# Two layers of windowed attention and a squared-ReLU MLP: products of scores and of maxima no longer ordered behind readers of other banks of their tile

## The chip, the core and the metric

The kernel runs on one core of a Trainium2 chip. The metric is the device time of one execution in microseconds (us), lower is better; three executions are shown for the kernel before, and profiled executions of its program give the views that are read here. Five engines work side by side, each through its own instructions in order: TensorE (PE, its weight loads shown apart as PEld), VectorE (DVE), ScalarE (ACT), GpSimd (POOL) and SyncE (SP), which here issues nearly all transfers. They wait for each other at semaphores.

## The reference

Input x has 2048 rows of 640. Four blocks follow each other: A, B, A, B, each added to x.

```
A: y = layernorm(x); q, k, v = split(y @ wqkv), 32 heads of 20
   s = (q @ k^T) * 20 ** -0.5, kept where 0 <= row - column < 256, else -1e9
   x = x + (softmax(s) @ v) @ wo
B: y = layernorm(x); h = relu(y @ w1 + b1); x = x + (h * h) @ w2 + b2     (w1: 640 x 1536)
```

Block A and block B of one pass are a layer of the kernel.

## The kernel before, in words

The 2048 rows are cut into 8 groups of 256 and there are two layers, so there are 16 units, numbered u in order; unit 8 is the first group of the second layer. The keys and values that a unit's rows may see are its own and those of the group before it. Units 0 and 8 have no group before them, and so have less attention work.

Products with weights (called dense here, all through `mm3`, L149) take each operand as a high and a low float16 part, and three products for each chunk of 128. They fill accumulators of one bank in the partial-sum memory (two buffers, tag `mm`), which ACT and DVE empty.

Attention goes by quads of four heads, eight quads a unit. Two kinds of turns use the other six banks, as two tiles of three banks (`banks`, tag `bb`, one for each half e of the partitions):

- A turn of maxima (`max_quad`, L282) forms the scores of a quad, 18 products (L308), and DVE adds the mask and takes row maxima in eight instructions (L321, a reduction and the read of its accumulator each). Banks 0, 1 and 2 hold w = 0, 1, 2; the products of w = 3 lie in the last 128 columns of all three banks, and are read last.
- A turn of scores (`exp_quad`, L345) forms the transposed scores less their maxima, 16 products (L359) in three steps, one bank of each tile for a step; ACT takes the exponential of each bank (L366, six a turn, into `pt`). GpSimd then clears what the window excludes (L376, L380). Units 0 and 8 have two steps and eight products.

Products of exponentials and values (`pv_quad`, L393, products L405) follow, in an `mm` buffer. ACT copies the result (L416), DVE and POOL divide by the sum, ACT and DVE split it in two parts `ot` (L426, L427), and SP writes these to memory (L431).

`together` (L547) writes out the order of TensorE by hand: for each quad a turn of scores, a share of dense products (0.55 of what belongs to the quad), a turn of maxima for a quad five further on, the products with the values, and the rest of the dense products. The dense products of an inner unit u are, in this order: q and k of unit u+1 (`stage_qk`), the output projection of unit u-1 (`stage_o`), v of unit u+1, and the MLP of unit u-1 (`stage_f`). TensorE keeps the order in which the program is written (L587). The order on the other engines is found by a scheduler that simulates the program, with some work preferred (`first`, L87).

Row maxima become rows of `qt` by way of a transpose on TensorE (L329), two DVE instructions and eight small transfers (L340). The normalised rows of `stage_o` become the left operand `y2` of the MLP by a cast on ACT (L214, `yl`), a subtraction on DVE (L215) and four transposing transfers (L217).

Dependencies between instructions are derived from the tiles that they touch. All products of a turn go into the same two tiles that ACT or DVE reads meanwhile.

## Time and profile before

| | us |
|---|---|
| median of three runs | 2677.45 |
| lowest, highest | 2673.51, 2682.87 |
| the profiled execution | 2666.85 |
| its span, first to last instruction | 2665.0 |
| TensorE busy in it | 2097.6 |
| VectorE, ScalarE, GpSimd busy | 1124.1, 810.4, 728.6 |

A busy time is the time in which at least one instruction of the engine runs. [...] Idle time of an engine is put down to whatever ended it. The first turn of scores of unit 0 starts at 119.2 us, and units 6, 8 and the last turn of scores are at 1026.1, 1348.6 and 2580.9 us.

### The profile page before, as it was taken

What the parts mean: (1) busy time and instruction counts of PE and PEld (TensorE: products, weight loads), DVE (VectorE), ACT (ScalarE), POOL (GpSimd) and SP (SyncE); (2) the same over time, 40 slices, a digit from 0 to 9 for tenths busy, and PEclk for the clock granted to TensorE, in tenths of its full rate; (3) what the DMA queues carried; (4) which work ended last, traced back from release to release, by engine and by line L of the source; (5) the groups of instructions that cost most, each with busy time, mean ns of one, the idle gap of its engine ahead of it and who ended that gap; (6) DMA issues with size and microseconds to landing.
All of it is one profiled execution on the core that took longest, in us unless ns stands there. A gap on an engine that the chain in (4) does not pass through costs nothing.

```text
span 2665.0 us, 45823 instructions
## 1 busy us (share of the span) xinstructions
PE 2097.6 (79%) x17542; PEld 1343.8 (50%) x17542; DVE 1124.1 (42%) x3473; ACT 810.4 (30%) x1716; POOL 728.6 (27%) x1434
## 2 busy tenths in 40 slices
PE   5777777877878788778888778787787877878688
PEld 4444445545554455445555555455544554545356
DVE  5554444343343443434445443434434334343422
ACT  5443223223232232332323232232322323223241
POOL 4333223223131231322322132231312223222241
PEclk9888888888888888888998888888888888888789
DMA  7540031130311302213141311403113022130100
GB/s 204 142 108 22 16 85 28 47 88 23 80 33 46 88 16 63 60 36 87 31 105 33 87 29 45 90 23 85 28 46 87 16 79 44 46 78 11 41 24 26
DMA packets 239069, 154.91 MB, mean 58 GB/s; under 512 B 80640, under 2 KB 219776, under 8 KB 238848
## 3 DMA queue, kind: packets, MB, share of 16 engines
q1 hardware_dynamic: 230432, 142.46, 21.8%
q10 hardware_dynamic: 8416, 9.51, 1.3%
q8 instruction: 138, 2.26, 0.4%
q14 instruction: 83, 0.68, 0.1%
HBM read 82.58 MB, written 52.43 MB: 51 GB/s over the span
## 4 chain that ended last, share of the span: by engine, by line
PE 61%; ACT 11%; DVE 10%; issue 9%; DMA 5%; SPq 3%; POOL 2%; ACTq 0%; DVEq 0%; POOLq 0%
PE acc L149 41%; PE pv L405 10%; ACT pt L366 7%; PE bb L359 5%; PE bb L308 4%; DVE bb L321 3%; SPq L340 2%; DVE mx L321 2%; DMA xt<-xs 1%; DMA stg<-in_B_w_dram 1%; ACT hh L497 1%; ACT r L493 1%; DVE bst L161 1%; ACT yl L214 1%; DMA stg<-in_A_wo_dram 1%
## 5 line engine op out<-in xcount | busy, mean ns | idle before, releaser
L321 DVE CUSTOM_DVE_ANT_0 bb<-bb,maskb 128x384 f32<-128x384 f32 (+2 forms) x1024 | 523.0, 559 | 301.4 <-PE bb L308 298.3
L366 ACT ACTIVATE pt<-bb 128x512 f32<-128x512 f32 x736 | 392.9, 586 | 206.5 <-PE bb L359 204.2
L308 PE MATMUL bb<-kt,qt 60*128 60x128 f16 (+1 forms) x2176 | 216.1, 245 | 272.9 <-DVE mx L321 270.0
L359 PE MATMUL bb<-qt,kt 62*128 62x128 f16 (+1 forms) x1920 | 212.8, 258 | 245.3 <-ACT pt L366 241.4
L423 POOL TENSOR_TENSOR po<-po,rb 128x256 f32<-128x256 f32 x128 | 93.2, 728 | 1117.9 <-DVE rb L422 1081.3
L149 PE MATMUL acc<-y,w_s 128*128 128x256 f16 x2880 | 388.2, 302 | 1.5 <-DVE y L176 1.5
L149 PE MATMUL acc<-w_s,hh 128*128 128x320 f16 x2304 | 372.4, 326 | 0.0
L149 PEld LDWEIGHTS <-w_s 128*128 128x128 f16 x2880 | 307.0, 109 | 98.0 <-issue 35.7
L416 ACT COPY po<-pv 128x256 f32<-128x256 f32 x128 | 47.6, 372 | 1010.6 <-PE pv L405 1010.6
L149 PE MATMUL acc<-yT,wq_s 128*128 128x256 f16 x2400 | 322.0, 301 | 5.4 <-DVE yT L176 3.0
L149 PEld LDWEIGHTS <-hh 128*128 128x128 f16 x2304 | 241.0, 106 | 136.3 <-issue 25.5
L149 PEld LDWEIGHTS <-wq_s 128*128 128x128 f16 x2400 | 252.8, 108 | 87.5 <-issue 38.5
L405 PE MATMUL pv<-pt,vt 128*32 128x128 f32 (+1 forms) x3840 | 293.9, 473 | 1.7 <-DVE qd L244 1.0
L308 PEld LDWEIGHTS <-qt 60*128 60x128 f16 x2176 | 95.3, 95 | 381.1 <-issue 378.8
L359 PEld LDWEIGHTS <-kt 62*128 62x128 f16 x1920 | 87.0, 94 | 357.5 <-issue 351.5
L376 POOL TENSOR_SCALAR_AFFINE_SELECT pt<-pt 128x256 f32<-128x256 f32 x448 | 187.9, 421 | 281.3 <-ACT pt L366 274.6
L380 POOL TENSOR_SCALAR_AFFINE_SELECT pt<-pt 128x256 f32<-128x256 f32 x512 | 207.8, 411 | 40.4 <-ACT pt L366 23.8
L498 DVE TENSOR_TENSOR hh<-r,hh 128x256 f16<-128x256 f32 x192 | 84.7, 458 | 259.9 <-ACT hh L497 253.1
L405 PEld LDWEIGHTS pv<-pt,vt 128*32 128x32 f32 x3840 | 149.1, 150 | 82.8 <-issue 67.2
L149 PE MATMUL acc<-wo_s,od 128*128 128x320 f16 x960 | 162.6, 332 | 5.6 <-DMA od<-o 3.9
L149 PE MATMUL acc<-wq_s,yT 128*128 128x320 f16 x960 | 160.8, 329 | 1.1 <-ACT vt L271 0.8
L496 POOL TENSOR_TENSOR r<-r 128x256 f32<-128x256 f32 x192 | 117.8, 634 | 156.2 <-ACT r L493 155.9
(62 smaller groups left out, 1449.6 us busy)
## 6 DMA issues: line engine op xcount, KB each, us to landing
qk<-qd SPq DMA_DIRECT2D x32, 640.0 KB
qt<-qk SPq DMA_DIRECT2D x32, 480.0 KB
kt<-qk SPq DMA_DIRECT2D x32, 480.0 KB
qk<-qd SPq DMA_DIRECT2D x32, 320.0 KB
o<-ot SPq DMA_DIRECT2D x256, 40.0 KB
od<-o SPq DMA_DIRECT2D x32, 320.0 KB
stg<-in_B_w_dram ACTq DMA_DIRECT2D x30, 256.0 KB
xt<-in_A_x_dram SPq DMA_DIRECT2D x16, 320.0 KB
```

The costliest lines, as they stand in the source:

```text
L149: nc.tensor.matmul(acc, lhs(a, c), rhs(b, c), start=(k == 0), stop=(k == 3 * nk - 1))
L308: nc.tensor.matmul(to, qt[r, p, i * P:(i + 1) * P], kt[r, p, a:b], start=True, stop=True)
L321: nc.vector.tensor_tensor_reduce(out=v, in0=v, in1=mask, scale=1.0, scalar=-3.0e38, op0=ALU.add, op1=ALU.max, accum_out=accum)
L340: nc.sync.dma_start(qt[r:r + 1, 2 * GQ * G:2 * GQ * (G + 1), i * P:(i + 1) * P], mT[s0:s0 + 2 * GQ, a, :])
L359: nc.tensor.matmul(bb[e][:, k, o:o + w], kt[r, 2 * qd + j, ko:ko + P], qt[r, 2 * qd + j, q0 * P:q0 * P + w], start=True, stop=True)
L366: at[0] = nc.scalar.activation(pt[:, :o], bb[e][:, k, :o], AF.Exp, scale=SCALE / (QS * QS))
L376: nc.gpsimd.affine_select(out=m, in_=m, pattern=[[0, 2], [-1, P]], compare_op=ALU.is_gt, fill=0.0, base=0, channel_multiplier=1)
L380: nc.gpsimd.affine_select(out=m, in_=m, pattern=[[0, 2], [1, P]], compare_op=ALU.is_ge, fill=0.0, base=0, channel_multiplier=-1)
L405: nc.tensor.matmul(pv[32 * jj:32 * (jj + 1), q0 * P:(q0 + qn) * P], vf[:, c:c + 32], pj[:, j, :], start=(k == 0), stop=(k == len(steps) - ...
L423: nc.gpsimd.tensor_tensor(po, po, rb.rearrange("p a b -> p (a b)"), op=ALU.mult)
L496: nc.gpsimd.tensor_tensor(r, r, r, op=ALU.mult)
L498: nc.vector.tensor_sub(hh[:, 1, f0 + f, :], r, hh[:, 0, f0 + f, :])
```

## The change

A helper `apart` tells the framework that a given product does not depend on a list of instructions. In both kinds of turns the kernel keeps a list `read` of the readers issued so far in this turn, and calls `apart` for each product that follows. The readers in the list work in other banks of the tile than the product; the readers of the product's own bank come after it in the program. Dependencies on the tile's previous user stay. No instruction is added or removed.

```
+    def apart(ins, others):
+        for it in others:
+            tc.declare_no_dep(ins.ins, it.ins, reason="other banks")
...
-        found = []
+        found, read = [], []
...
-                    nc.tensor.matmul(to, qt[r, p, i * P:(i + 1) * P], kt[r, p, a:b], start=True, stop=True)
+                    apart(nc.tensor.matmul(to, qt[r, p, i * P:(i + 1) * P], kt[r, p, a:b], start=True, stop=True),
+                          read)
...
-                nc.vector.tensor_tensor_reduce(out=v, in0=v, in1=mask, scale=1.0, scalar=-3.0e38,
-                                               op0=ALU.add, op1=ALU.max, accum_out=accum)
+                read.append(nc.vector.tensor_tensor_reduce(out=v, in0=v, in1=mask, scale=1.0, scalar=-3.0e38,
+                                                           op0=ALU.add, op1=ALU.max, accum_out=accum))
...
-        out = []
+        out, read = [], []
...
-                        nc.tensor.matmul(bb[e][:, k, o:o + w], kt[r, 2 * qd + j, ko:ko + P],
-                                         qt[r, 2 * qd + j, q0 * P:q0 * P + w], start=True, stop=True)
+                        apart(nc.tensor.matmul(bb[e][:, k, o:o + w], kt[r, 2 * qd + j, ko:ko + P],
+                                               qt[r, 2 * qd + j, q0 * P:q0 * P + w], start=True, stop=True), read)
...
+                read.append(at[0])
```

TensorE's instructions stand in the same order before and now; only what they wait for differs. This is a turn of scores of a unit with three steps, from the last product of the first step to the first of the third; `Activation_49` is the semaphore of ACT. Before:

```order
L359 MATMUL bb<-qt,kt_79 128x256
L359 LDWEIGHTS kt_79
L359 MATMUL bb<-qt,kt_79 128x128 [waits Activation_49]
L359 LDWEIGHTS kt_79
L359 MATMUL bb<-qt,kt_79 128x128 [waits Activation_49]
...
L359 MATMUL bb<-qt,kt_77 128x128
L359 LDWEIGHTS kt_77
L359 MATMUL bb<-qt,kt_77 128x256 [waits Activation_49]
L359 LDWEIGHTS kt_77
L359 MATMUL bb<-qt,kt_77 128x256 [waits Activation_49]
```

The same products now:

```order
L365 MATMUL bb<-qt,kt_79 128x256
L365 LDWEIGHTS kt_79
L365 MATMUL bb<-qt,kt_79 128x128
L365 LDWEIGHTS kt_79
L365 MATMUL bb<-qt,kt_79 128x128
...
L365 MATMUL bb<-qt,kt_77 128x128
L365 LDWEIGHTS kt_77
L365 MATMUL bb<-qt,kt_77 128x256
L365 LDWEIGHTS kt_77
L365 MATMUL bb<-qt,kt_77 128x256
```

The four waits for ACT inside the turn are gone; the waits of the first products of the turn, for the readers of the tiles' last user, stand as they did. In a turn of maxima four waits for DVE go in the same way.

The other engines' instructions are the same in number, and stand in part in another order. On ACT, in the fourth turn of scores of unit 7 (its exponentials are `pt_11788` to `pt_11817`), before:

```order
L416 COPY po_11719<-pv_11701 128x256
L426 CAST ot_11718<-po_11719 128x2x128
L214 CAST yl_11751<-xt_11642 128x640
L271 ACTIVATE vt4_92<-acc_11760 128x16x20
L366 ACTIVATE pt_11788<-bb_11782 128x512
L366 ACTIVATE pt_11791<-bb_11783 128x512
L214 CAST yl_11751<-xt_11741 128x640
L366 ACTIVATE pt_11802<-bb_11782 128x512
L366 ACTIVATE pt_11806<-bb_11783 128x512
L366 ACTIVATE pt_11814<-bb_11782 128x512
L366 ACTIVATE pt_11817<-bb_11783 128x512
```

And now:

```order
L423 COPY po_11719<-pv_11701 128x256
L214 CAST yl_11751<-xt_11642 128x640
L271 ACTIVATE vt4_92<-acc_11760 128x16x20
L372 ACTIVATE pt_11788<-bb_11782 128x512
L372 ACTIVATE pt_11791<-bb_11783 128x512
L433 CAST ot_11718<-po_11719 128x2x128
L372 ACTIVATE pt_11802<-bb_11782 128x512
L372 ACTIVATE pt_11806<-bb_11783 128x512
L372 ACTIVATE pt_11814<-bb_11782 128x512
L372 ACTIVATE pt_11817<-bb_11783 128x512
L214 CAST yl_11751<-xt_11741 128x640
```

The second cast of `yl` moved from behind two of the six exponentials to behind all six, and the cast of `ot` from ahead of them to behind the first two. On SP, the queue of transfers of one unit, before:

```order
L217 DMA_TRANSPOSE y2_8590<-yl_8591 128x5x128 x2
L466 DMA xt_8779<-in_B_b2_dram 128x640
L217 DMA_TRANSPOSE y2_8590<-yl_8591 128x5x128 x2
L340 DMA qt_6495<-mT_8662 1x8x128 x8
...
L431 DMA o5_8176<-ot_8558 20x2x512 x4
L217 DMA_TRANSPOSE yT_9241<-yl_9242 128x5x128 x2
L431 DMA o5_8176<-ot_8970 20x2x512 x4
L217 DMA_TRANSPOSE yT_9241<-yl_9242 128x5x128 x2
```

And now:

```order
L217 DMA_TRANSPOSE y2_8590<-yl_8591 128x5x128 x2
L473 DMA xt_8779<-in_B_b2_dram 128x640
L346 DMA qt_6495<-mT_8662 1x8x128 x4
L217 DMA_TRANSPOSE y2_8590<-yl_8591 128x5x128 x2
L346 DMA qt_6495<-mT_8662 1x8x128 x4
...
L438 DMA o5_8176<-ot_8558 20x2x512 x4
L217 DMA_TRANSPOSE yT_9241<-yl_9242 128x5x128 x3
L438 DMA o5_8176<-ot_8970 20x2x512 x4
L217 DMA_TRANSPOSE yT_9241<-yl_9242 128x5x128
```

Four of the eight transfers of maxima now stand ahead of the second pair of transposes and four behind it, and one more transpose stands ahead of the second write of `ot`.

## Rows read from the trace of the kernel before

**Rows 1.** The page: busy time, share of the span and instructions of each engine.
```profile
PE 2097.6 (79%) x17542; PEld 1343.8 (50%) x17542; DVE 1124.1 (42%) x3473; ACT 810.4 (30%) x1716; POOL 728.6 (27%) x1434
```
**Rows 2.** Span and mean granted TensorE clock of the core.
```profile
core 0: 2665.0 us, clock 0.851
```
**Rows 3.** Waits: who waited for whom, us in total, times, longest.
```profile
PE bb L308 <- DVE mx L321: 270.0, 486, 4.3
...
PE bb L359 <- ACT pt L366: 241.4, 455, 3.3
```
**Rows 4.** Timeline, a turn of scores: start, us, engine, line, xcount, idle before.
```profile
1213.84 0.39 PE L359 MATMUL bb<-qt,kt 62*128 62x256 f16 x4
...
1214.32 1.08 ACT L366 ACTIVATE pt<-bb 128x512 f32<-128x512 f32 x2 [1.01 <-PE bb L359]
1214.97 0.21 PE L359 MATMUL bb<-qt,kt 62*128 62x128 f16 x1 [0.74 <-ACT pt L366]
...
1215.46 0.38 PE L359 MATMUL bb<-qt,kt 62*128 62x128 f16 x7 [0.28 <-ACT pt L366]
...
1216.55 0.27 PE L359 MATMUL bb<-qt,kt 62*128 62x256 f16 x1 [0.71 <-ACT pt L366]
...
1217.03 0.38 PE L359 MATMUL bb<-qt,kt 62*128 62x256 f16 x3 [0.22 <-ACT pt L366]
```
**Rows 5.** Timeline, a turn of maxima on TensorE and VectorE, first and last rows.
```profile
1224.03 0.51 PE L308 MATMUL bb<-kt,qt 60*128 60x128 f16 x10
1224.57 0.57 DVE L321 CUSTOM_DVE_ANT_0 bb<-bb,maskb 128x384 f32<-128x384 f32 x1 [1.84 <-PE bb L308]
...
1228.59 0.60 DVE L321 CUSTOM_DVE_ANT_0 bb<-bb,maskb 128x384 f32<-128x384 f32 x1
...
1229.10 0.60 DVE L321 CUSTOM_DVE_ANT_0 bb<-bb,maskb 128x384 f32<-128x384 f32 x1
```
**Rows 6.** Windows: busy us (x) of PE, PEld, DVE, ACT, POOL; clock, DMA share, GB/s.
```profile
1213.84:1217.34 3.50, 1.55 (x17) 0.71 (x17) 0.00 (x0) 2.17 (x4) 1.53 (x4) 1.00 0.86 280
1217.34:1221.10 3.76, 3.76 (x21) 2.74 (x21) 0.00 (x0) 1.08 (x2) 1.59 (x5) 0.55 0.54 127
1221.10:1224.02 2.92, 2.92 (x27) 2.44 (x25) 0.69 (x1) 0.60 (x1) 0.00 (x0) 1.00 1.06 169
0.00:119.20 119.20, 76.64 (x532) 52.88 (x532) 61.86 (x219) 54.53 (x106) 44.50 (x50) 0.91 0.65 177
1026.10:1194.30 168.20, 134.56 (x1127) 85.60 (x1126) 70.67 (x214) 48.58 (x102) 43.62 (x90) 0.84 0.23 54
1348.60:1391.10 42.50, 36.23 (x334) 25.89 (x335) 22.67 (x81) 11.81 (x26) 7.53 (x17) 1.00 0.54 135
1348.60:1479.00 130.40, 107.91 (x909) 73.40 (x908) 65.64 (x214) 36.56 (x86) 31.70 (x58) 0.92 0.31 70
2580.90:2665.00 84.10, 76.99 (x601) 57.45 (x600) 19.30 (x44) 14.97 (x36) 14.58 (x23) 0.97 0.11 34
```
**Rows 7.** The same view of line L308 alone: busy us of PE, PEld; clock.
```profile
1224.02:1227.53 3.51, 1.56 (x18) 0.76 (x18) 1.00 0.03 4
```
**Rows 8.** Timeline of TensorE about the start of unit 8.
```profile
1343.28 1.51 PE L405 MATMUL pv<-pt,vt 128*32 128x256 f32 x32
1344.72 3.98 PE L149 MATMUL acc<-w_s,hh 128*128 128x320 f16 x28
...
1364.66 5.09 PE L149 MATMUL acc<-yT,wq_s 128*128 128x256 f16 x45
```
**Rows 9.** Timeline of ACT ahead of a turn of scores that starts at 1314.62 us.
```profile
1312.55 0.84 ACT L493 ACTIVATE r<-acc,b1s 128x256 f32<-128x256 f32 x2 [1.89 <-PE acc L149]
...
1315.44 1.09 ACT L366 ACTIVATE pt<-bb 128x512 f32<-128x512 f32 x2
```
**Rows 10.** Waits of SP's queue: us in total, times, longest.
```profile
SPq L217 <- ACT hh L497: 373.2, 9, 43.4
```

## The prediction

> **What bounds the kernel now.** I read the shares of busy time first: TensorE is busy for 2097.6 of 2665.0 us, VectorE for 42%, ScalarE for 30% [rows 1]. So TensorE sets the time, and two things can be had from it: the 567.4 us in which it stands idle, and the clock at which it works, which is 0.851 in the mean [rows 2].

> The list of waits says where the idle time lies: 270.0 us in products of maxima that wait for VectorE, in 486 waits, and 241.4 us in products of scores that wait for ScalarE, in 455 [rows 3]. Together that is 511.4 us; 56.0 us are left for everything else. A turn of scores in the timeline shows what these waits are [rows 4]. Four products run, then the next waits 0.74 us for the first exponential and the one behind it 0.28 us for the second; then the third step waits 0.71 and 0.22 us in the same way. That is 1.95 us of idle time in a turn of 3.5 us. A unit of three steps has eight such turns with four waits each, and the number of waits fits these inner ones alone. In front of the turns there is nothing: from 1221.10 to 1224.02 TensorE is busy throughout [rows 6], and the turn of maxima starts at 1224.03 [rows 5].

> The windows show the second cost [rows 6]. In the turn of scores the clock is granted in full, 1.00, and TensorE is busy for 1.55 of 3.50 us. [...] Unit 8 is the counter-example that the kernel brings along: its turns of scores have two steps, its first turns of maxima are shorter too, TensorE is busy for 36.23 of the first 42.50 us, and the clock is 1.00 throughout. So I read the fall of the clock as a consequence of the idle time in the turns.

> **The change part by part.** The order of TensorE is the same, and the rows of the order show the four inner waits of a turn gone. Inside a turn a product then has nothing to wait for, and the 511.4 us go as far as nothing else is late in their place.

> For the clock I rebuild a unit of three steps from rows at clock 1.00. Dense products by the code: 10 groups of 15 for q and k and 12 of 15 for the first half of the MLP make 330 of 256 columns; 8 groups of 15 for v and the output projection and 4 of 36 for the second half make 264 of 320 columns. A product of 256 columns takes 5.09 / 45 = 0.113 us and one of 320 columns 3.98 / 28 = 0.142 us [rows 8], so 37.3 + 37.5 = 74.8 us. Eight turns of scores at 1.55 us [rows 6], eight of maxima at 1.56 us [rows 7] and eight products with the values at 1.51 us [rows 8] add 37.0 us. That makes 111.8 us, where unit 6 has 134.56 us of busy TensorE at a clock of 0.84, in 168.20 us [rows 6]. The ratio is 0.831.

> Over the kernel: 76.64 us of busy time belong to the start, 107.91 to unit 8 and 76.99 to the end, whose clocks of 0.91, 0.92 and 0.97 leave less to win [rows 6]. At clock 0.84 a fall of 0.16 is worth 16.9% of the busy time; in proportion 0.09 is worth 9.5%, 0.08 8.4% and 0.03 3.2%, so these become 69.4, 98.8 and 74.5 us. The other 1836.1 us times 0.831 make 1525.8. TensorE's work at the upper level is thus about 1768.5 us. With the 56.0 us of other idle time the span would be 1824.5 us if nothing else came late.

> What comes late next is the tail of the readers, which now runs into the dense work behind the turn. ScalarE: its first exponential starts 0.48 us after the turn, and six at 0.54 us [rows 4] end 3.7 us after it. The next turn of maxima needs their banks after 1.55 us of products and 0.55 of 74.8 / 8, that is 5.1 us of dense work: at 6.7 us. VectorE: its first reduction starts 0.54 us after the turn's first product and they follow each other every 0.51 us [rows 5], so eight end after about 4.7 us; the next turn of scores comes after 1.56 + 1.51 + 4.2 = 7.3 us. These 3.0 and 2.6 us of dense work are the cover. What can use it up is other work in the same queues. In unit 6 VectorE is busy for 70.67 us, of which 64 reductions take 33; ScalarE for 48.58, of which 48 exponentials take 26 [rows 6]. That leaves 4.7 and 2.8 us of other work for each quad. If all of it fell into the tails, VectorE would be 4.7 + 4.7 - 7.3 = 2.1 us late and ScalarE not at all: 16.8 us a unit. The lower bound is 0.

> The moved casts on ScalarE I cost at nothing: the dense work between turns hides them. Of the cast of `yl` that now stands behind four more exponentials, the cover is v of the next unit; if that is too short, the transposes behind it, `y2`, and the four transfers of maxima queued behind these on SP are late by up to 4 x 0.54 = 2.2 us each, once a unit: 4.4 us more. So a unit loses between 0 and 21 us to new waits. I take 5, nearer to the lower end, because the rows show no wait ahead of a turn today and the cover of 2.6 us is above half of the other work of VectorE. Over 16 units that is 80 us.

> The sum: 1824.5 + 80 = 1904.5 us of span. The profiled execution is 1.85 us above its span, and the median of the runs is 0.47% above this span; I scale by that to 1913, and forecast 1915 us. With 0 and 21 us a unit it is 1833 and 2171 us.

> [...]

> **The rivals.** First: only the waits go, and the clock stays as it is. For it: the mean clock also contains falls behind turns of maxima and products with the values, and those I have not taken apart. Against it: unit 8. Its time: 2097.6 + 56.0 + 80 = 2234 us of span, 2244 us.

> Second: the waits come back at the first product of a turn. One mechanism: ScalarE and VectorE work in order, and other work stands ahead of the readers. For it: at 1312.55 ScalarE begins with the MLP and reaches the exponentials of a turn at 1315.44, 2.9 us later and 0.8 us after the turn's start [rows 9]. Against it: the cover of 2.6 to 3.0 us. At the upper bound the time is 2171 us; with some falls of the clock kept as well, about 2200.

> Third, slower than before: SP's queue. One more transpose now stands ahead of a write of `ot`; `ot` has a single buffer, so a late write holds ScalarE's next cast, and the exponentials behind it. SP waits for such transposes by as much as 43.4 us, nine times 373.2 us in total [rows 10]. Were TensorE to pay 43.4 us in each of 12 units, 521 us would more than cancel the waits, and idle TensorE would lose the clock too: about 2690 us. It decides once SP is held for longer than the quad, some 14 us, between a write of `ot` and the next. Against it: transposes stood ahead of these writes before, and TensorE has next to no wait that leads back to them.

> That the change does nothing is excluded by the rows of the order.

> **How the numbers follow.** The forecast, waits gone and the clock up, with 0 to 14 us of new waits a unit (1833 to 2060 us), has 0.76. The second rival has 0.12, about half of it below 2170; the first 0.09; the third 0.03. The range of 1835 to 2170 us leaves out some 0.18. A measurement of this kernel tells 0.3% from no change. All but the third rival are faster, so 0.97 for faster; of its 0.03 I give 0.01 to no change and 0.02 to slower.

> **What would show it.** Right: the two waits fall from 511.4 us to under 100, what is left stands at the first products of turns, a turn of scores takes about 1.6 us, the mean clock is above 0.95, and an inner unit takes about 117 us. Only the clock wrong: turns of 1.6 us, but windows at 0.5 remain. The tails wrong: a list of waits in which the same two pairs keep hundreds of us. The third: TensorE waiting for `po`, `pt` or `kt` by tens of us at a time. A time above 2244 us would refute the whole argument.

## The result, and the profile after

The changed kernel takes 1794.42 us (median of four runs), the kernel before 2675.48 us (median of four): a ratio of 0.6705, with a 95% interval of 0.6687 to 0.6723. That is a third less time, in the direction that was forecast, and below the range that was given (1835 to 2170 us). The profiled execution has a span of 1792.0 us. One later execution of the changed kernel (2688.47 us, its clock held at 0.558) and one of the kernel before (6120.37 us) are left out of the medians and ratios below.

The page of the changed kernel, its row of engines:

```profile
PE 1616.1 (90%) x17542; PEld 1177.0 (66%) x17542; DVE 1068.6 (60%) x3473; ACT 781.2 (44%) x1716; POOL 742.0 (41%) x1434
```

Its clock, in the view that answers to [rows 2]:

```profile
core 0: 1792.0 us, clock 0.979
```

The list of waits of TensorE (us in total, times, longest us):

```profile
PE acc L149 <- DVE qd L244: 23.9, 29, 1.6
PE bb L365 <- DVE mx L327: 20.2, 23, 2.5
PE acc L149 <- DMA od<-o: 17.0, 3, 9.3
...
PE pv L412 <- ACT r L500: 10.5, 14, 1.5
...
PE bb L365 <- DVE rc L428: 7.7, 16, 1.9
...
PE bb L313 <- ACT pt L372: 4.0, 5, 1.8
```

The two pairs that held 511.4 us [rows 3] are gone: no product of scores waits for an exponential of its own turn, and no product of maxima for a reduction of its own turn. What is left stands at first products (20.2 + 7.7 us for VectorE's tail, 4.0 us for ScalarE's, and 0.9 us between turns of maxima at the start), in front of the products with the values and in the dense work. TensorE's idle time is 1792.0 - 1616.1 = 175.9 us, where it was 567.4.

The timeline of TensorE and of ScalarE through one quad of an inner unit; these rows answer to [rows 4], [rows 5] and [rows 8]:

```profile
519.04 0.83 PE L365 MATMUL bb<-qt,kt 62*128 62x256 f16 x16
519.81 4.79 PE L149 MATMUL acc<-wo_s,od 128*128 128x320 f16 x34
524.53 0.84 PE L313 MATMUL bb<-kt,qt 60*128 60x128 f16 x18
525.30 1.51 PE L412 MATMUL pv<-pt,vt 128*32 128x256 f32 x32
526.74 1.67 PE L149 MATMUL acc<-wo_s,od 128*128 128x320 f16 x11
```

```profile
519.53 3.04 ACT L372 ACTIVATE pt<-bb 128x512 f32<-128x512 f32 x6 [0.77 <-PE bb L365]
```

There is no bracket of idle time on TensorE's rows: the pieces join. The 16 products of scores take 0.83 us and the 18 of maxima 0.84 us. ScalarE's six exponentials end at 522.57, 3.53 us after the turn's start and 1.96 us ahead of the next turn: the tail lies under dense work, as the sum had it (3.7 us).

Windows of the changed kernel, columns as in [rows 6]; they are the start, units 0, 1 and 2, then unit 6, unit 8, the turns of unit 15, and the end:

```profile
0.00:110.30 110.30, 68.81 (x532) 49.90 (x532) 59.55 (x222) 53.73 (x106) 43.31 (x50) 0.90 0.71 194
110.30:176.90 66.60, 51.41 (x504) 33.02 (x504) 40.27 (x132) 38.88 (x89) 35.18 (x56) 0.90 0.43 121
176.90:279.00 102.10, 82.48 (x926) 57.39 (x925) 57.53 (x195) 40.78 (x93) 41.43 (x87) 0.90 0.13 33
279.00:387.10 108.10, 101.46 (x1124) 74.08 (x1124) 68.10 (x218) 46.89 (x102) 45.27 (x91) 0.98 0.34 83
...
702.70:808.80 106.10, 99.26 (x1125) 73.06 (x1125) 67.17 (x214) 46.89 (x102) 45.04 (x91) 1.00 0.37 85
...
911.20:1004.80 93.60, 89.89 (x909) 66.92 (x908) 61.47 (x214) 34.95 (x85) 32.58 (x57) 1.00 0.41 96
...
1635.00:1709.20 74.20, 55.15 (x629) 36.13 (x629) 34.17 (x105) 34.19 (x79) 36.13 (x77) 0.89 0.12 33
1709.20:1792.00 82.80, 75.51 (x600) 56.24 (x599) 20.87 (x47) 17.83 (x44) 17.57 (x29) 1.00 0.11 35
```

Unit 6 took 168.20 us at a clock of 0.84 [rows 6] and takes 106.10 us at 1.00, with TensorE busy for 99.26 us of it. The start, units 0 to 2 and unit 15 still lose clock (0.90, 0.90, 0.90, 0.98 and 0.89); the other units have 1.00.

Where the 873 us of span went is read from TensorE's groups (line, count, busy us, mean ns, idle before). After:

```profile
L149 PE MATMUL acc<-y,w_s 128*128 128x256 f16 x2880 | 337.4, 275 | 13.5 <-ACT r L500 8.5 <-DMA y<-yl 2.8 <-DVE y L176 1.5
L149 PE MATMUL acc<-w_s,hh 128*128 128x320 f16 x2304 | 325.7, 299 | 0.0
L149 PE MATMUL acc<-yT,wq_s 128*128 128x256 f16 x2400 | 286.5, 278 | 14.8 <-DVE qd L244 9.8 <-DVE yT L176 3.7 <-ACT po L423 1.3
L412 PE MATMUL pv<-pt,vt 128*32 128x128 f32 (+1 forms) x3840 | 194.2, 332 | 20.1 <-ACT r L500 10.5 <-POOL pt L387 7.4 <-DVE qd L244 1.7
L149 PE MATMUL acc<-wo_s,od 128*128 128x320 f16 x960 | 143.2, 305 | 32.4 <-DMA od<-o 17.0 <-DVE qd L244 13.7 <-DVE x L465 1.7
L149 PE MATMUL acc<-wq_s,yT 128*128 128x320 f16 x960 | 142.9, 300 | 16.3 <-DVE mT L339 14.7 <-ACT vt L271 1.1 <-DVE qd L244 0.3
L365 PE MATMUL bb<-qt,kt 62*128 62x128 f16 (+1 forms) x1920 | 108.3, 246 | 27.9 <-DVE mx L327 20.2 <-DVE rc L428 7.7
L313 PE MATMUL bb<-kt,qt 60*128 60x128 f16 (+1 forms) x2176 | 105.2, 237 | 5.6 <-ACT pt L372 4.0 <-DVE mx L327 0.9 <-DMA kt<-qk 0.6
```

The same groups of the kernel before:

```profile
L149 PE MATMUL acc<-y,w_s 128*128 128x256 f16 x2880 | 388.2, 302 | 1.5 <-DVE y L176 1.5
L149 PE MATMUL acc<-w_s,hh 128*128 128x320 f16 x2304 | 372.4, 326 | 0.0
L149 PE MATMUL acc<-yT,wq_s 128*128 128x256 f16 x2400 | 322.0, 301 | 5.4 <-DVE yT L176 3.0 <-DVE qd L244 2.4
L405 PE MATMUL pv<-pt,vt 128*32 128x128 f32 (+1 forms) x3840 | 293.9, 473 | 1.7 <-DVE qd L244 1.0 <-ACT r L493 0.7
L308 PE MATMUL bb<-kt,qt 60*128 60x128 f16 (+1 forms) x2176 | 216.1, 245 | 272.9 <-DVE mx L321 270.0 <-DVE bmv L163 1.1 <-DMA kt<-qk 0.4
L359 PE MATMUL bb<-qt,kt 62*128 62x128 f16 (+1 forms) x1920 | 212.8, 258 | 245.3 <-ACT pt L366 241.4 <-DMA qt<-mT 0.5 <-issue 0.2
L149 PE MATMUL acc<-wo_s,od 128*128 128x320 f16 x960 | 162.6, 332 | 5.6 <-DMA od<-o 3.9 <-DVE x L458 1.7
L149 PE MATMUL acc<-wq_s,yT 128*128 128x320 f16 x960 | 160.8, 329 | 1.1 <-ACT vt L271 0.8 <-DVE qd L244 0.3
```

| TensorE, us | before | after | less |
|---|---|---|---|
| idle | 567.4 | 175.9 | 391.5 |
| products of scores and maxima (two rows) | 428.9 | 213.5 | 215.4 |
| products with the values | 293.9 | 194.2 | 99.7 |
| dense (five rows) | 1406.0 | 1235.7 | 170.3 |

The rows add to 876.9; they overlap a little where groups join. The third and fourth rows, 270.0 us, I put down to the clock: in unit 6 the dense products and those with the values were busy for 86.98 and 21.74 us at a mean clock of 0.84, and are for 75.83 and 12.15 us at 1.00. The second row is not idle time, and only a part of it is the clock (the eight interrupted turns of scores of unit 6 took 14.33 us at its clock of 0.84, about 1.8 us each; the pieces of the turn in [rows 4], which ran at 1.00, add to 1.63 us). It is the one that the prediction had wrong.

### The profile page after: what moved, and what is told of

Read it like the earlier page. It is cut to its first block, busy times and chain, and to the rows that moved or that the text cites. A ratio compares the mean times of both kernels' runs of the same rounds, so it can differ in the third digit from the quotient of the medians.

```text
span 1792.0 us, 45770 instructions
## 1 busy us (share of the span) xinstructions
PE 1616.1 (90%) x17542; PEld 1177.0 (66%) x17542; DVE 1068.6 (60%) x3473; ACT 781.2 (44%) x1716; POOL 742.0 (41%) x1434
## 4 chain that ended last, share of the span: by engine, by line
PE 53%; DVE 19%; issue 8%; POOL 8%; ACT 6%; DMA 5%; SPq 1%; ACTq 0%; DVEq 0%; POOLq 0%
PE acc L149 41%; DVE bb L327 8%; PE pv L412 4%; ACT pt L372 4%; PE bb L365 3%; DVE mx L327 3%; PE bb L313 3%; POOL pt L387 2%; POOL pt L383 2%; DVE hh L505 2%; POOL r L503 2%; DMA qk<-qd 1%; DVE rb L426 1%; POOL po L430 1%; DVE qd L244 1%
## 5 line engine op out<-in xcount | busy, mean ns | idle before, releaser
L327 DVE CUSTOM_DVE_ANT_0 bb<-bb,maskb 128x384 f32<-128x384 f32 (+2 forms) x1024 | 512.6, 558 | 126.4 <-PE bb L313 125.3
L149 PE MATMUL acc<-y,w_s 128*128 128x256 f16 x2880 | 337.4, 275 | 13.5 <-ACT r L500 8.5
L149 PEld LDWEIGHTS <-w_s 128*128 128x128 f16 x2880 | 278.1, 98 | 75.0 <-issue 38.6
L149 PE MATMUL acc<-w_s,hh 128*128 128x320 f16 x2304 | 325.7, 299 | 0.0
L149 PE MATMUL acc<-yT,wq_s 128*128 128x256 f16 x2400 | 286.5, 278 | 14.8 <-DVE qd L244 9.8
L412 PE MATMUL pv<-pt,vt 128*32 128x128 f32 (+1 forms) x3840 | 194.2, 332 | 20.1 <-ACT r L500 10.5
L412 PEld LDWEIGHTS pv<-pt,vt 128*32 128x32 f32 x3840 | 107.9, 110 | 70.9 <-issue 28.2
L433 ACT CAST ot<-po 128x256 f16<-128x256 f32 x128 | 52.3, 408 | 228.9 <-POOL po L430 228.9
L149 PEld LDWEIGHTS <-od 128*128 128x128 f16 x960 | 92.5, 99 | 81.2 <-issue 28.0
L327 DVE DVE_READ_ACCUMULATOR2_ANT mx<- 128x1 f32 x1024 | 143.6, 140 | 0.0
L365 PE MATMUL bb<-qt,kt 62*128 62x128 f16 (+1 forms) x1920 | 108.3, 246 | 27.9 <-DVE mx L327 20.2
```

The costliest lines, as they stand in the source:

```text
L149: nc.tensor.matmul(acc, lhs(a, c), rhs(b, c), start=(k == 0), stop=(k == 3 * nk - 1))
L327: read.append(nc.vector.tensor_tensor_reduce(out=v, in0=v, in1=mask, scale=1.0, scalar=-3.0e38, op0=ALU.add, op1=ALU.max, accum_out=accum))
L365: apart(nc.tensor.matmul(bb[e][:, k, o:o + w], kt[r, 2 * qd + j, ko:ko + P], qt[r, 2 * qd + j, q0 * P:q0 * P + w], start=True, stop=True), ...
L412: nc.tensor.matmul(pv[32 * jj:32 * (jj + 1), q0 * P:(q0 + qn) * P], vf[:, c:c + 32], pj[:, j, :], start=(k == 0), stop=(k == len(steps) - ...
L433: nc.scalar.copy(oh, pf)
```

## The experiments

**One kind of turn alone.** The theory was that each interrupted turn costs its own waits and its own fall of the clock; the rival, that one interrupted turn a quad holds the clock down as much as two. The first run leaves `apart` away in the turns of maxima:

```
-                    apart(nc.tensor.matmul(to, ...), read)
+                    nc.tensor.matmul(to, ...)
```

> Only the turns of scores lose their inner waits; the turns of maxima wait as before. Theory (idle time in the turns, its pipeline tails, and a clock that falls behind each interrupted turn): the 241 us of waits for ScalarE go, the busy time of these products falls from 213 to about 108 us, and half of the 270 us that dense products and products with the values lost to the clock comes back: 2675 - 241 - 105 - 135, plus some 60 us of new waits, about 2255 us, mean clock about 0.92. Rival (one interrupted turn a quad holds the clock down as much as two): the clock stays near 0.85 and the time near 2390 us.

Measured: 2189.76 us, clock 0.908. The second leaves it away in the turns of scores:

```
-                        apart(nc.tensor.matmul(bb[e][:, k, o:o + w], ...), read)
+                        nc.tensor.matmul(bb[e][:, k, o:o + w], ...)
```

> Only the turns of maxima lose their inner waits. Theory: 270 us of waits for VectorE and about 111 us of busy time of these products go, and half of the clock's 270 us: 2675 - 270 - 111 - 135 + 60, about 2220 us, mean clock about 0.92. Rival (one interrupted turn a quad is enough for the clock): about 2355 us at a clock near 0.85. If the two halves of the change were independent, the savings of this run and of the one with scores alone would add to 881 us.

Measured: 2237.77 us, clock 0.900. Both are within 3% of the theory and 5 to 9% from the rival, and both clocks are nearer to the theory's 0.92 than to 0.85. Against 2669.82 us for the kernel before beside them they save 480 and 432 us, 912 together, where the whole change saves 881: nearly independent. TensorE's groups show which turn takes the clock from which work. With the turns of scores freed:

```profile
L411 PE MATMUL pv<-pt,vt 128*32 128x128 f32 (+1 forms) x3840 | 275.5, 444 | 6.5 <-POOL pt L386 5.0 <-DVE qd L244 1.0 <-POOL pt L382 0.3
L313 PE MATMUL bb<-kt,qt 60*128 60x128 f16 (+1 forms) x2176 | 214.2, 242 | 280.8 <-DVE mx L326 273.8 <-ACT pt L371 3.8
...
L364 PE MATMUL bb<-qt,kt 62*128 62x128 f16 (+1 forms) x1920 | 102.7, 245 | 0.5 <-issue 0.3
```

With the turns of maxima freed:

```profile
L365 PE MATMUL bb<-qt,kt 62*128 62x128 f16 (+1 forms) x1920 | 219.2, 260 | 297.9 <-ACT pt L372 274.0 <-DVE rc L428 9.7 <-DVE mx L327 6.5
L412 PE MATMUL pv<-pt,vt 128*32 128x128 f32 (+1 forms) x3840 | 184.7, 331 | 1.8 <-DVE qd L244 0.7 <-POOL pt L387 0.6 <-ACT r L500 0.5
...
L313 PE MATMUL bb<-kt,qt 60*128 60x128 f16 (+1 forms) x2176 | 106.3, 240 | 2.2 <-DVE mx L327 1.2 <-DMA kt<-qk 0.8
```

The products with the values stand right behind the turn of maxima: they stay at 275.5 us while that turn is interrupted and fall to 184.7 when it is not. The five dense groups, which stand behind both, add to 1279.6 us in the first run and 1370.3 in the second, between 1406.0 and 1235.7. So I read from these busy times that the clock falls behind the turn that idles, and comes back with it (0.908 and 0.900 in the mean, where it is 0.851 with both turns interrupted and 0.979 with none). The busy time of a turn's own products halves in the run that frees it, and only there (scores 102.7 and 219.2 us, maxima 214.2 and 106.3).

**Idle time without waits.** If idle time is what costs, it can be filled in place of being removed. This kernel has all the dependencies of the kernel before, and puts dense products between the steps of a turn:

```
+            if w < 2:
+                between(1.5e3)
...
+            if k + 1 < len(steps):
+                between(1.5e3)
...
+            fill[0] = None if after and k == 0 else more
```

Here `between` draws 1.5 us from the same generator of dense products that fills the time behind the turns. The first turn of scores of each unit, and the turns of maxima at the start, are left whole.

> The kernel before with all its dependencies, but 1.5 us of dense products are put between the steps of a turn (not in the first turn of scores of a unit), and taken from the dense work behind the turns. Theory (it is TensorE's idle time in the turns that costs, by itself and by the clock, not the dependencies as such): the readers work under the dense products, the inner waits nearly go, the clock is above 0.95 and the time is near that of the changed kernel: 1830 us (1780 to 1900). Rival (the waits cost by being there, as semaphores or through the order of the other engines): it stays above 2400 us.

Measured: 1956.67 us, clock 0.963. The rival is out, but the time is 57 us above the end of the theory's range. Its groups of turns:

```profile
L367 PE MATMUL bb<-qt,kt 62*128 62x128 f16 (+1 forms) x1920 | 180.0, 252 | 82.3 <-DVE mx L327 40.1 <-ACT pt L374 32.5 <-DMA qt<-mT 3.9
L314 PE MATMUL bb<-kt,qt 60*128 60x128 f16 (+1 forms) x2176 | 158.8, 240 | 30.9 <-DVE mx L327 17.2 <-ACT pt L374 11.7 <-DMA kt<-qk 0.8
```

The 32.5 us for ScalarE lie mostly in the first turns of scores of the units, which have no dense products in them. TensorE is idle for 195.7 us in this run (1956.0 - 1760.3), hardly more than in the changed kernel, but the products of the turns are busy for 338.8 us instead of 213.5. One of its turns of maxima, at a clock of 1.00 and with no wait in it:

```profile
704.18 0.51 PE L314 MATMUL bb<-kt,qt 60*128 60x128 f16 x10
...
706.84 0.34 PE L314 MATMUL bb<-kt,qt 60*128 60x128 f16 x4
...
708.86 0.34 PE L314 MATMUL bb<-kt,qt 60*128 60x256 f16 x4
```

The three pieces add to 1.19 us, where the whole turn takes 0.84: 0.18 us a break. In [rows 4] the five pieces add to 1.63 us, against 0.83 for the whole turn: 0.20 us a break. Over the kernel I counted pieces in the traces, a piece ending where other products follow or where TensorE stands idle: the turns are in 1202 pieces before, 280 after and 851 here. So a further piece costs 215.4 / 922 = 0.23 us before, with part of the lower clock in it, and 125.3 / 571 = 0.22 us here. My reading is that each piece has a start and an end that the next one does not share, and that breaking the turn pays them again. These are busy times of the turns' own products; where a piece joins dense work the two overlap (by 0.06 us at 519.81 us of the changed kernel: 519.04 + 0.83 - 519.81), so TensorE's own row grows by 144.2 us (1760.3 against 1616.1), the lower clock (0.963 against 0.979) included. How much of that is breaks and how much clock is not shown.

**Halves.** At the rate of the dense products, 0.113 us for 256 columns [rows 8], the 3072 columns of a turn would take 1.36 us one behind the other, by this estimate; the turn takes 0.83, and the next work starts 0.77 us after the turn's start (519.81 - 519.04). The two halves e use different partitions, so I took it that they run side by side because they alternate; in the records of this turn the 16 products start in eight pairs, the two of a pair 3 to 5 ns apart. On this theory the forecast for halves that do not alternate was about 1920 us (1880 to 1950); by the estimate above, 1.36 - 0.83 = 0.53 us more in some 240 turns make 127 us, and with the 1794 us of the changed kernel 1921 us. The first run puts e outside within each step:

```
-                for j in range(2):
-                    for e in range(2):
...
+            for e in range(2):
+                o = 0
...
+                    for j in range(2):
```

> As the changed kernel, but in a turn all products of the half e = 0 come before those of e = 1, instead of alternating. Same products, same columns. [...] Rival (the turn is short only because no product waits any more and the modelled ends are counted once): no change, 1794 us within 10.

Measured: 1798.17 us: the rival's number. But it does not show the rival's reason (the profile models the ends of TensorE's products). The turn in its timeline:

```profile
568.15 0.84 PE L313 MATMUL bb<-kt,qt 60*128 60x128 f16 x18
```

It is as short as before, and still shorter than the 1.36 us of its columns in a row. In the records of this turn the first products of the two halves start 10 ns apart, although two or three of one half stand in the program ahead of the other's each time. Over the kernel the turns are busy for 111.2 and 106.3 us, against 108.3 and 105.2. To tell the two apart the halves had to be further from each other. The next two runs write all products of a turn ahead of all its readers, with no dependency declared away; the second sorts them by half:

```
+        items = [(w, part, e) for w in (3, 0, 1, 2) for part in parts_of(w)[3] for e in range(2)]
+        items.sort(key=lambda it: it[2])        # second run alone
+        for w, (kt, a, b, c), e in items:
...
+            nc.tensor.matmul(to, qt[r, p, i * P:(i + 1) * P], kt[r, p, a:b], start=True, stop=True)
+        for w in (3, 0, 1, 2):                  # then the readers, as before
```

> The kernel before, without any call that takes a dependency away, but written so that all products of a turn come first and all its readers after them. The products stand on TensorE in the order of the changed kernel. Theory (the inner waits came only from readers that stand in the program ahead of later products of the same tile): no reader stands ahead of a product, the waits are gone, and the time is that of the changed kernel, 1794 us, plus up to 30 us if the first reader now waits for the last product (0.35 to 0.4 us later in each turn, mostly under dense work). Rival (the waits would come back another way, at the readers): above 2000 us.

For the second there were two forecasts, both against the first. Theory (with eight or nine products of one half ahead of the other's, the halves no longer run side by side): turns near the 1.36 us, and 60 to 150 us more. Rival (they run side by side over a whole turn): turns of 0.85 us, and the same time within 10 us.

> As the run with all products of a turn first, but all products of the half e = 0 of the turn stand ahead of those of e = 1. To be read against that run. In the run with the halves apart within a step alone, the trace showed the first products of both halves starting 10 ns apart, so the two halves ran side by side all the same. [...]

Measured: 1811.83 us and 1837.66 us. The first says that the order in which the program is written was the cause of the waits: written products first, the kernel before is 17 us from the changed one, with no dependency taken away. The second, timeline of a turn of maxima with one half behind the other:

```profile
572.19 1.18 PE L311 MATMUL bb<-kt,qt 60*128 60x128 f16 x18
```

1.18 us, 0.34 more than with the halves alternating, and less than the 1.36 of the columns in a row: by that estimate the halves overlap in part even there. The time grows by 26 us, which is neither the theory's 60 to 150 nor the rival's 10: part of the longer turns falls into time in which TensorE would have waited (idle 141.3 us against 181.2).

**The cover of the tails.** The share of dense work behind the turn of scores, 0.55, sets how much of it covers ScalarE's tail and how much VectorE's.

```
-    SHARE = 0.55
+    SHARE = 0.75        # other runs: 0.30, 0.45
```

> The changed kernel with 0.75 instead of 0.55 of a quad's dense work behind the turn of scores, so only 0.25 behind the turn of maxima. Theory (dense work is the cover of the readers' tails): behind a turn of maxima there are 0.84 + 1.51 + 0.25 x 9.4 = 4.7 us of TensorE, and VectorE's reductions alone end after about 4.7; with its other work it is 1 to 2 us late in some 112 turns, so the time is 1900 to 2020 us, and the waits of scores for maxima (20 us) grow to over 100. Rival (the tails are far from deciding): within 15 us of 1794.

> The changed kernel with 0.30 of a quad's dense work behind the turn of scores. Theory (cover): ScalarE's exponentials end about 3.7 us after the turn's start and TensorE comes to the turn of maxima after 0.84 + 0.30 x 9.4 = 3.7 us; with ScalarE's other work it is up to 1.5 us late, and the products with the values, which need GpSimd's part too, wait as well: 1850 to 1980 us. Rival (not deciding): within 15 us of 1794.

Measured: 1899.48 us at 0.75, and 1800.19 us at 0.30. TensorE's waits at 0.75:

```profile
PE bb L365 <- DVE mx L327: 83.5, 107, 3.0
PE bb L365 <- DVE rc L428: 52.0, 60, 3.4
```

And at 0.30:

```profile
PE pv L412 <- POOL pt L387: 35.6, 18, 2.8
PE pv L412 <- DVE qd L244: 18.7, 14, 2.6
PE bb L313 <- ACT pt L372: 16.7, 40, 1.5
```

VectorE's cover decides, as the theory had it, with a time at the lower end of its range (1900 to 2020 us): with less cover, turns of scores wait 135.5 us. For ScalarE the rival was right (within 15 us of 1794), and the theory wrong by 50 us and more: at 0.30 the turns of maxima wait 16.7 us in all, so ScalarE's other work seldom makes its tail late; what begins to wait are the products with the values, for GpSimd and VectorE.

**A version that beats both.** With both ends known, a share in between, and more of the last unit's dense work spread over its turns, where TensorE is busy for 55.15 of 74.20 us:

```
-        together(quads, ahead, dense, cost, 0.6 if last else 1.0, not last, ...)
+        together(quads, ahead, dense, cost, 0.8 if last else 1.0, not last, ...)
```

> The changed kernel once more, as the measure for the two runs beside it: 1794 us within 5 us.

> The changed kernel with 0.45 of a quad's dense work behind the turn of scores. Theory (VectorE's tail is the one that is short of cover at 0.55, 28 us of waits in front of turns of scores; the products with the values are the ones short of it at 0.30, 60 us): both are covered in between, and 10 to 25 us go: 1770 to 1785 us. Rival (the waits only move): 1794 us within 5.

> As the run with 0.45, and 0.8 instead of 0.6 of the last unit's dense work is spread over its turns. Theory (the last unit's turns have too little dense work beside them: TensorE is busy for 55 of 74 us there, at a clock of 0.885): 5 to 12 us less than with 0.45 alone. Rival (what is taken from the end is only moved): no difference beyond 4 us.

Measured: 1795.55 us for the changed kernel, 1785.18 us at 0.45 and 1779.89 us with the last unit's 0.8 as well; ratios to the kernel before 0.6703 (0.6684 to 0.6723), 0.6667 (0.6648 to 0.6687) and 0.6651 (0.6630 to 0.6671). The share is worth 10.4 us, at the low end of what was expected; the intervals overlap a little, but no run at 0.45 (1783.65 to 1787.02 us) is as long as any at 0.55 (1791.97 to 1796.33). The theory holds for VectorE's tail only. At 0.45 the products with the values are not covered:

```profile
PE pv L412 <- POOL pt L387: 23.7, 25, 2.5
...
PE pv L412 <- ACT r L500: 16.0, 14, 1.6
```

For the last step of 5.3 us the runs of the two kernels overlap: it points to a gain, and I do not call it shown. In the profiled executions, one of each, the stretch from the first turn of scores of unit 15 to the end takes 157.2 us at 0.6 (1781.9 - 1624.7) and 151.6 us at 0.8 (1778.9 - 1627.3), which is where the theory put the gain.

## Why the prediction was wrong

**The waits.** Right. The 511.4 us of inner waits went, in the places named; the runs with one kind of turn each show that their removal did it.

**The clock.** Right, and the first rival with it refuted: the clock is 0.979 (above 0.95 was asked for), and the two single runs show it come back by turns. By the sum, dense products and products with the values in an inner unit were to take 74.8 and 12.1 us; the windows of these lines alone in unit 6 of the changed kernel give 75.83 and 12.15 us. The profile before shows single microseconds at 0.50 and at 1.00, here two of the dense work behind the turn of [rows 4], columns as in [rows 6]:

```profile
1219.00:1220.00 1.00, 1.00 (x6) 0.71 (x5) 0.00 (x0) 0.00 (x0) 0.04 (x1) 0.50 0.70 194
...
1223.00:1224.00 1.00, 1.00 (x11) 0.73 (x8) 0.00 (x0) 0.00 (x0) 0.00 (x0) 1.00 0.96 141
```

The longest gap on TensorE in that turn is 0.74 us [rows 4], and the clock of the 3.76 us behind it is 0.55 [rows 6]. With the gaps gone, unit 6 has 1.00 throughout.

**The products of a turn.** This is the step that failed: "Eight turns of scores at 1.55 us [rows 6], eight of maxima at 1.56 us [rows 7]". I took the busy time of an interrupted turn for that of an uninterrupted one. Unit 6 of the changed kernel, windows of these two lines alone (busy us of PE and PEld, then the clock), scores first:

```profile
702.70:808.80 106.10, 6.92 (x128) 4.45 (x129) 1.00 0.37 85
```

```profile
702.70:808.80 106.10, 6.69 (x144) 4.71 (x144) 1.00 0.37 85
```

That is 0.87 and 0.84 us a turn, where the sum has 12.4 and 12.5 us a unit: 11.3 us too much in each inner unit. It explains most of the 152.4 us by which TensorE's work was put too high (1768.5 against 1616.1 us). The rows would have told it: in [rows 4] four products of 256 columns take 0.39 us and a single one 0.27, so three more cost 0.12 us. So most of the 0.27 us is not columns, and the sum of the five pieces contained it five times. The clock was not in this, since the turns of [rows 6] and [rows 7] ran at 1.00. The ratio of 0.831 carried the error on to the other units: there TensorE is busy for 1381.9 us (1616.1 - 68.81 - 89.89 - 75.51) where the sum has 1525.8, which is 143.9 of the 152.4 us; the start (68.81 against 69.4) and the end (75.51 against 74.5) were about right, and unit 8 has the rest (89.89 against 98.8).

**New waits.** Right in the inner units that were read, and too low over the kernel. For unit 6 the sum has 5 us of new waits, and all its idle time is 106.10 - 99.26 = 6.84 us. Over the kernel the idle time came to 175.9 us instead of 136 (56.0 + 80). The start has 110.30 - 68.81 = 41.5 us of it, but that stood there before (119.20 - 76.64 = 42.6 us). The units that were put too low are 0, 1 and 15, which are idle for 15.2, 19.6 and 19.1 us. Among these are a wait of 9.3 us in unit 1 and one of 7.5 us in unit 15 for `od`, which I had not looked at. So the two errors are -152.4 and +39.9 us, together the -112.5 us between 1904.5 and 1792.0; the second hides part of the first.

**The range.** Its lower end was the sum with no new waits at all, and so took the price of the turns as certain. An estimate for them was in reach: 0.27 us for the first 256 columns of [rows 4] and 0.04 us for each of the eleven times 256 that follow are 0.71 us a turn.

**The rivals.** The second did not come: turns wait 27.9 + 5.6 us at their starts. Its condition is real, as the run at 0.75 shows, with VectorE as the engine. The third did not come: no wait of TensorE names `po`, `kt` or `pt` by tens of us. The nearest to it are the three waits for `od`, which is read from where the writes of `ot` go: 17.0 us, where the kernel before has 3.9.

## What to carry to other kernels

In this kernel short waits inside a burst on TensorE cost three times: the waits themselves (511.4 us), the start and end of the piece that each breaks off (about 0.2 us a break, counted as busy), and the clock of the work behind (0.55 behind the turn of [rows 4], 1.00 in unit 6 without such waits). Before pricing a burst without its waits, compare a group of n products with a single one in the timeline, and do not take the busy time of the broken burst. Where a tile spans several banks, look in the list of waits for products that wait for readers of another bank; writing all products ahead of their readers did nearly the same here as declaring them independent (1811.83 and 1794.42 us).
